# Constant rows written in 32-bit words on two engines, quotients of every head on ScalarE, and a newly searched order

## Chip, cores and metric

The kernel runs on one core of one Trainium2 chip. The metric is the device time of one execution in microseconds; of several runs the median counts. Engines are named TensorE (PE; PEld for its weight loads), VectorE (DVE), ScalarE (ACT), GpSimd (POOL) and SyncE (SP, which issues all the DMAs here). L448 means line 448 of the kernel before.

## What is computed

Eight batches of eight attention heads (1152 keys of 64 columns; queries averaged in pairs, so 576), followed by a channel mix with token shift on the 512 columns of each batch:

```python
q_pool = q.reshape(B, H, S // 2, 2, D).mean(axis=3)
scores = scale * np.matmul(q_pool, k.transpose(0, 1, 3, 2))
scores = scores - np.max(scores, axis=-1, keepdims=True)
attn = np.exp(scores); attn = attn / (np.sum(attn, axis=-1, keepdims=True) + 1e-09)
x = np.matmul(attn, v)                          # then heads side by side: (B, 576, 512)
...
xk = mu_k * x + (1.0 - mu_k) * x_prev
xr = mu_r * x + (1.0 - mu_r) * x_prev
k = np.maximum(xk @ w_k, 0.0)
v = k * k @ w_v
r = 1.0 / (1.0 + np.exp(-(xr @ w_r)))
return (r * v)
```

All is float32 outside; inside, each factor is a float16 value and a float16 remainder, so a product takes two or three matmuls.

## The kernel before

**Tiling.** The 64 heads (`n`) run one after the other, each in six blocks (`j`) of 96 queries against all 1152 keys (nine chunks of 128). A block computes scores into one of three PSUM banks `s` (L602), finds a maximum for each query on VectorE (for heads 0 to 13 in `row`, L612 to L622; from head 14 on in `top` and `join`, L627 to L648), adds the remainder products and the maximum (L653), takes exponentials on ScalarE into `pf` (L660) and has GpSimd make a scaled half-word copy `pl` (L663). `halves` (L712) and `window` (L741 to L748) multiply by the values into the one PSUM bank `a`. At the last window of a head the sums are divided: VectorE adds a guard and takes reciprocals (L764, L766), and the quotients `xb` are written by ScalarE for the first eight heads, one operation for each 128 queries (L769), and by one VectorE operation for the others (L773). After each second head the pair is turned: by a DMA transpose (`crossed`, L791 to L802) or on TensorE (`turns`, L818). When the eight heads of a batch are done, `mix` (L953 to L964) and `ff` (L985 to L1052) compute the channel mix in tiles of 256 tokens.

**Key buffers.** `ks1` holds, for each head, the keys and their remainders, turned; `ks2` (two buffers, used by even and odd heads) holds the keys once more in rows 64 to 127, copied there by a DMA (L551). Its rows 0 to 63 are written once, at the start: zeros, and two constants in rows 0 and 1, which multiply the maximum of a query.

**Order.** No engine works in program order of the source. Every operation is given to `op(engine, duration, function, reads, writes, key)`. A planner plays all of them with these durations and hand-over times, by key, refines the order in rounds, and then applies nudges (`MOVES`): each takes a centre in planned time, a width and a share of the operations there, and shifts their priorities. The result is one fixed order for each engine. The durations are used for the order alone. What stands outside `op` (identity, mask, gather, the fills of L442 to L456) is issued ahead of all that, in source order on its engine. SyncE's queue is in order, too: a DMA that waits holds those behind it.

The lines that the change and the steps below touch: the fills of `ks2` (L447 to L450), of `md` (L446), the casts into `gather` (L390), the subtraction for the key remainders (L540), the first query sums (L486), the quotients (L767 to L775), and the names `X_ACT`, `MOVES`, `SEED`, `GA`.

Of the kernel before, what the change touches and what calls it, by code (L numbers as in the profile page):

```python
# [4 lines left out]

# [6 lines left out]
F32 = mybir.dt.float32  # L12
# [27 lines left out]
CROSS = range(4, 31)  # L40
N_ROW = 14
PAIR = 99
GA = 0.045
XM = 3
SPLIT_ENG = 'ACT'
JOIN_ENG = 'ACT'
# [32 lines left out]
VB_DVE = 0  # L79
WHI_DVE = 0  # L80
VB_DUR = 0.25
X_ACT = 8
K_ONE = 2
Q_ONE = 2
N_QN = 2
# [2 lines left out]
WDEP = [("ks1", 1), ("ks2", 0), ("vr", 1)]  # L88
AHEAD2 = 0
MOVES, BASE, REACH = (  # L90
    34, 51, 119, 147, 174, 176, 191, 263, 328, 478, 600, 742, 785, 805, 941, 956, 1439, 1609, 3150, 4342,
    5377, 6334, 7410, 9224, 10224, 10571, 13731, 15873, 16751, 17268, 19136, 22188, 24107, 24376, 25583,
    25931, 31593,
), 2000000, 1150.0
SEED, SPREAD = 7, 1.0


class Issue:
# [224 lines left out]
def kernel(  # L323
# [63 lines left out]
    for a in range(P // U):  # L387
        part = slice(a * U, (a + 1) * U)
        nc.vector.memset(mask[part, a + 1:a + 2], 1.0 / SM)
        nc.gpsimd.tensor_copy(gather[part], ident[part, part].unsqueeze(1).broadcast_to([U, P // U, U]))  # L390
    nc.vector.memset(mask[0:U, 0:1], 1.0 / SM)

    kr, vr = bufs("kr", 2, [P, NC, D], F32), bufs("vr", 2, [P, NC, D], F32)
# [48 lines left out]
        nc.gpsimd.memset(t_[:, 1, :, 0:D], 0.0)  # L442
    for t_ in mx:
        nc.vector.memset(t_[:, 0:P - QN], 0.0)
    for t_ in md:
        nc.gpsimd.memset(t_, 0.0)  # L446
    for t_ in ks2:  # L447
        nc.vector.memset(t_[0:D], 0.0)  # L448
        nc.vector.memset(t_[0:2], -SM * 2.0 * EPS)
        nc.vector.memset(t_[0:1], -SM * (1.0 - EPS))  # L450
    for t_ in vt:
        nc.vector.memset(t_[:, :, 2 * D:2 * D + 2], 1.0)
    for t_ in vb:
# [128 lines left out]
    def block(n, j, i, t):  # L582

        hp, z = n % 2, i % 3
        qi = n // 2 % 2
        q0 = hp * TQ + j * QN
        qhi, qlo = (qT[qi][:, r].rearrange("p j x -> p (j x)")[:, q0:q0 + QN] for r in (0, 1))
        kh, kl = ([(t_, qi, c) for c in range(q0 // P, (q0 + QN - 1) // P + 1)] for t_ in ("qT", "qTl"))
        qm = [("qm", qi, q0)]
        s = s_b[z]  # L590
        p0 = (0 if hp else HW) + j * QN
        rows, us = slice(p0, p0 + QN), range(p0 // U, (p0 + QN) // U)

        def cols(c0, c1):
            return s[:, P + c0 * QN:P + c1 * QN]

        def grid(c0, c1):
            return cols(c0, c1).rearrange("p (c q) -> p c q", q=QN)

        def scores(c0, c1):  # L600
            for c in range(c0, c1):
                nc.tensor.matmul(cols(c, c + 1), ks1[hp][:, c, :], qhi,  # L602
                                 start=(c == c0), stop=False, skip_group_check=True)

        def first():
            for c0, c1 in BK:
                op("PE", (c1 - c0) * 0.0430, lambda c0=c0, c1=c1: scores(c0, c1),
                   r=[("ks1", hp), ("ks1", hp, 5)] + kh, w=[("s", z)], key=t)

        def row():  # L610
            mxz, mbz, y = mx[i % 2], mb[z], i % 2
            op("DVE", 0.975, lambda: nc.vector.tensor_reduce(mxz[:, P - QN:P], grid(0, NC).rearrange("p c q -> p q c"),  # L612
                                                             axis=AX.X, op=ALU.max),
               r=[("s", z)], w=[("mx", y)], key=t)
            op("PE", 0.059, lambda: nc.tensor.matmul(s[:, 0:P], mxz, identb, start=False, stop=False, skip_group_check=True),
               r=[("mx", y)], w=[("s", z)], key=t + O_MAX)
            op("DVE", 0.199, lambda: nc.vector.tensor_reduce(mbz, s[:, 0:P], axis=AX.X, op=ALU.max),
               r=[("s", z)], w=[("mb", z)], key=t + O_MAX)
            op("PE", 0.047, lambda: nc.tensor.matmul(s[:, 0:QN], mbz.broadcast_to([P, P]), negi[:, P - QN:P],
                                                     start=False, stop=False, skip_group_check=True),  # L620
               r=[("mb", z)], w=[("s", z)], key=t + O_MAX)
            op("ACT", 0.153, lambda: nc.scalar.activation(qlo[0:1], s[0:1, 0:QN], getattr(AF, ROW),  # L622
                                                          scale=(1.0 + EPS) / (1.0 - EPS), alpha=(1.0 - EPS) / (1.0 + EPS)),
               r=[("s", z)] + kl, w=qm, key=t + O_MAX)

        def top(y, a):
            op("DVE", 0.972, lambda: nc.vector.tensor_reduce(  # L627
                my[y][:, a], cols(0, NC).rearrange("p (x q) -> p x q", q=U), axis=AX.X, op=ALU.max, apply_transpose=True),
               r=[("s", z)], w=[("my", y)], key=t)

        def join(y, m):
            ql = qT[qi][0:U, 1].rearrange("p j x -> p (j x)")[:, q0 + QN - m * QN:q0 + QN]
            kls = kl if m == 1 else [("qTl", qi, c) for c in range((q0 - QN) // P, (q0 + QN - 1) // P + 1)]
            qms = [("qm", qi, q0 - x * QN) for x in range(m)]
            mr, got = s[:, 0:3 * m], s[0:U, U:U + 18 * m].rearrange("p (j k) -> p j k", k=6)
            mqz = mq[y][:, 0:3 * m]
            op("DVE", 0.062 + 0.028 * m, lambda: nc.vector.tensor_reduce(
                mr.rearrange("p (a j) -> p a j", j=3), my[y][:, 0:m].rearrange("p a (c j) -> p a j c", j=3), axis=AX.X, op=ALU.max),
               r=[("my", y)], w=[("s", z)], key=t + O_MAX)
            op("DVE", 0.061 + 0.019 * m, lambda: nc.vector.tensor_tensor(  # L640
                mqz, mr.unsqueeze(2).broadcast_to([P, 3 * m, 6]), mask.unsqueeze(1).broadcast_to([P, 3 * m, 6]), op=ALU.mult),
               r=[("s", z)], w=[("mq", y)], key=t + O_MAX)
            op("PE", GA, lambda: nc.tensor.matmul(s[:, U:U + 18 * m], gather.rearrange("p a x -> p (a x)"),
                                                  mqz.rearrange("p j k -> p (j k)"), start=False, stop=False, skip_group_check=True),
               r=[("mq", y)], w=[("s", z)], key=t + O_MAX)
            op("DVE", 0.055 + 0.031 * m, lambda: nc.vector.tensor_reduce(
                md[y][:, 0:3 * m, 0:2], windows(got, 5), axis=AX.X, op=ALU.max), r=[("s", z)], w=[("md", y)], key=t + O_MAX)
            op("DVE", 0.072 + 0.1 * m, lambda: nc.vector.transpose(ql, md[y][:, 0:3 * m].rearrange("p j x -> p (j x)")),  # L648
               r=[("md", y)] + kls, w=qms, key=t + O_MAX)

        def scores2(c0, c1):
            for c in range(c0, c1):
                nc.tensor.matmul(cols(c, c + 1), ks2[hp][:, c, :], qlo,  # L653
                                 start=False, stop=True, skip_group_check=True)

        def second():
            for c0, c1 in BK:
                op("PE", (c1 - c0) * 0.0430, lambda c0=c0, c1=c1: scores2(c0, c1),
                   r=[("ks2", hp)] + kl + qm, w=[("s", z)], key=t + O_EXP)
            op("ACT", NC * QN / 1200 + 0.06, lambda: nc.scalar.activation(  # L660
                pf[:, :, rows], grid(0, NC), AF.Exp, bias=SHIFT, scale=0.125 / (2.0 * SQ)),
               r=[("s", z)], w=[("pf", x) for x in us] + [("gate", i)], key=t + O_EXP)
            op("POOL", NC * QN / 1000 + 0.12, lambda: nc.gpsimd.tensor_scalar(  # L663
                pl[:, :, rows], half(pf, U16, 0)[:, :, rows], LO, 1.0, op0=ALU.mult, op1=ALU.mult),
               r=[("pf", x) for x in us], w=[("pl", x) for x in us], key=t + O_REST, port=True)

        return first, row, top, join, second

# [59 lines left out]
    def window(n, w, t):  # L728
# [37 lines left out]
        op("DVE", 0.08, lambda: nc.vector.reciprocal(dz, dz), r=[("den", z)], w=[("den", z)], key=t + O_EVAC)  # L766
        if n < X_ACT:  # L767
            for k_ in range(nk):
                op("ACT", 0.051 + D / 1200, lambda k_=k_: nc.scalar.activation(  # L769
                    xb[0][:, 2 * (k0 + k_) + hh], u[:, k_, 0:D], AF.Copy, scale=dz[:, k_:k_ + 1]),  # L770
                   r=[("den", z), ka], w=[("xb", 2 * (k0 + k_) + hh)], key=t + O_EVAC)
        else:
            op("DVE", 0.07 + nk * D / 960, lambda: nc.vector.tensor_tensor(  # L773
                xb[0][:, 2 * k0 + hh:2 * NW:2], u[:, :, 0:D], dz.unsqueeze(2).broadcast_to([P, nk, D]), op=ALU.mult),
               r=[("den", z), ka], w=[("xb", 2 * k_ + hh) for k_ in range(k0, NW)], key=t + O_EVAC)  # L775
# [2 lines left out]

    def copier(e, n):

        return {"POOL": (0.12 + n * 0.00113, nc.gpsimd.tensor_copy), "ACT": (0.093 + n / 1200, nc.scalar.copy),
                "DVE": (0.07 + n / 960, nc.vector.tensor_copy)}[e]

    def crossed(b, g, t):
# [268 lines left out]
        return key  # L1053


    queries(0, -20.0)
    prep(0, -20.0)
    prep(1, -10.0)
# [76 lines left out]
```

## Time and profile before

| | |
|---|---|
| median of 3 runs | 1095.19 us (1095.1 to 1096.24) |
| profiled execution | 1096.61 us, its span 1094.8 us |
| busy: TensorE, VectorE, ScalarE, GpSimd | 1052.2, 920.7, 878.2, 593.6 us |
| mean granted clock of TensorE | 0.995 |
| moved by DMA | 134.52 MB, mean 123 GB/s |

The span runs from the first to the last instruction of the profiled execution; the rest of its time lies around it. "Busy" of an engine is the time in which at least one of its instructions was under way. A row of a group gives busy time, mean duration, and after the second bar the idle time of the engine just before the group's instructions with what ended it ("<-").

### The profile page before, as it was taken

The numbers are of one execution on the slowest core, as the hardware profiler recorded it, in microseconds if no ns is written. First come the engines' busy times: TensorE is split into PE (matmuls) and PEld (weight loads), VectorE is DVE, ScalarE is ACT, GpSimd is POOL, SyncE is SP. The second block draws the span as 40 slices with busy tenths as digits, with TensorE's granted clock in tenths as the row PEclk, the third lists the DMA queues.
The fourth block names the chain that finished last, engine by engine and source line by source line (L and its number), as shares of the span: only waits on it lengthen the run. The fifth ranks groups of instructions, "written<-read, shape, count | busy, mean of one in ns | idle before, by whom it ended". The sixth has DMA issues, their size and how long they took to land.

```text
span 1094.8 us, 43933 instructions
## 1 busy us (share of the span) xinstructions
PE 1052.2 (96%) x18521; PEld 858.5 (78%) x18521; DVE 920.7 (84%) x2400; ACT 878.2 (80%) x1604; POOL 593.6 (54%) x641
## 2 busy tenths in 40 slices
PE   5888899999999999999999999999999999999998
PEld 4777887978688887888787888878787978787565
DVE  8889888989899989998998998998889899975321
ACT  6999998978778888888887788887788887865643
POOL 3556685645555464654565465656465645554431
PEclk9999999999999999999999999999999999999999
DMA  8998955666666538674675655565656654510000
GB/s 204 234 233 201 192 131 130 140 142 111 134 124 121 123 71 179 128 132 79 143 157 100 143 125 124 122 141 113 134 113 130 143 116 89 90 40 12 20 28 22
DMA packets 254166, 134.52 MB, mean 123 GB/s; under 512 B 189456, under 2 KB 226320, under 8 KB 253968
## 3 DMA queue, kind: packets, MB, share of 16 engines
q1 hardware_dynamic: 253968, 131.71, 57.6%
q8 instruction: 145, 2.38, 0.9%
q14 instruction: 53, 0.43, 0.1%
HBM read 67.11 MB, written 9.44 MB: 70 GB/s over the span
## 4 chain that ended last, share of the span: by engine, by line
PE 82%; ACT 5%; DVE 5%; DMA 2%; issue 2%; POOL 0%; ACTq 0%; DVEq 0%
PE f L985 34%; PE s L602 11%; PE s L653 11%; PE a L748 5%; PE a L743 5%; PE a L741 5%; PE s L985 5%; ACT pf L660 2%; PE a L712 2%; PE a L985 2%; DMA ks<-kn 2%; DVE my L627 1%; ACT xt L802 1%; DVE mx L612 1%; DVE xm L956 1%
## 5 line engine op out<-in xcount | busy, mean ns | idle before, releaser
L663 POOL TENSOR_SCALAR pl<-pf 128x864 f16<-128x864 uint16 x384 | 384.3, 1001 | 360.0 <-ACT pf L660 322.4
L660 ACT ACTIVATE pf<-s 128x864 int32<-128x864 f32 x384 | 335.1, 887 | 89.2 <-PE s L653 40.2
L627 DVE TRANSPOSE_TENSOR_REDUCE my<-s 128x27 f32<-128x864 f32 x300 | 319.9, 1072 | 48.7 <-PE s L602 35.9
L602 PE MATMUL s<-qT,ks 128*128 128x96 f16 x3456 | 216.7, 207 | 11.7 <-ACT pf L660 10.6
L653 PE MATMUL s<-qT,ks 128*128 128x96 f16 x3456 | 211.5, 207 | 3.8 <-ACT qT L622 2.9
L602 PEld LDWEIGHTS <-ks 128*128 128x128 f16 x3456 | 181.5, 98 | 41.4 <-issue 16.0
L653 PEld LDWEIGHTS <-ks 128*128 128x128 f16 x3456 | 177.6, 98 | 26.8 <-issue 5.1
L743 PE MATMUL a<-vt,pf 128*128 128x64 f16 x2304 | 192.0, 194 | 0.4 <-issue 0.4
L741 PE MATMUL a<-vt,pf 128*128 128x65 f16 x2304 | 191.5, 193 | 0.4 <-DVE xb L773 0.4
L741 PEld LDWEIGHTS <-pf 128*128 128x128 f16 x2304 | 160.1, 99 | 4.6 <-issue 0.7
L743 PEld LDWEIGHTS <-pf 128*128 128x128 f16 x2304 | 154.7, 98 | 6.4 <-issue 1.2
L985 PE MATMUL f<-xhk,wk_hi 128*128 128x256 f16 x496 | 135.0, 272 | 0.0
L985 PE MATMUL f<-xlk,wk_hi 128*128 128x256 f16 x496 | 135.0, 272 | 0.0
L985 PE MATMUL f<-xhk,wk_lo 128*128 128x256 f16 x496 | 135.0, 272 | 0.0
L748 PE MATMUL a<-vb,pl 128*128 128x65 f16 x2304 | 122.8, 193 | 0.1
L985 PEld LDWEIGHTS <-wk_hi 128*128 128x128 f16 x1152 | 105.0, 98 | 11.5 <-issue 0.5
L1016 POOL TENSOR_TENSOR gl<-g 128x512 f16<-128x512 f32 x72 | 78.9, 1097 | 55.5 <-ACT g L1014 53.6
L748 PEld LDWEIGHTS <-pl 128*128 128x128 f16 x2304 | 97.3, 98 | 6.0 <-POOL pl L663 0.3
L612 DVE TENSOR_REDUCE mx<-s 128x96 f16<-128x864 f32 x84 | 87.3, 1052 | 16.3 <-PE s L602 5.6
L985 PE MATMUL f<-wv_hi,g 128*128 128x512 f16 x240 | 90.8, 378 | 2.1 <-ACT ex L1033 2.0
L985 PE MATMUL f<-wv_lo,g 128*128 128x512 f16 x240 | 90.9, 379 | 0.0
L985 PE MATMUL f<-wv_hi,gl 128*128 128x512 f16 x240 | 90.9, 379 | 0.0
(130 smaller groups left out, 2095.1 us busy)
## 6 DMA issues: line engine op xcount, KB each, us to landing
kr<-in_k_dram SPq DMA_DIRECT2D x64, 288.0 KB
vr<-in_v_dram SPq DMA_DIRECT2D x64, 288.0 KB
qr<-in_q_dram SPq DMA_DIRECT2D x63, 256.0 KB
ks<-ks SPq DMA_DIRECT2D x64, 144.0 KB
out_dram<-em SPq DMA_DIRECT2D x36, 256.0 KB
xt<-in_moe_w_k_dram SPq DMA_DIRECT2D x8, 512.0 KB
xt<-in_moe_w_v_dram SPq DMA_DIRECT2D x8, 512.0 KB
qr<-in_q_dram SPq DMA_DIRECT2D x32, 64.0 KB
```

Source lines behind the costliest of these rows:

```text
L602: nc.tensor.matmul(cols(c, c + 1), ks1[hp][:, c, :], qhi, start=(c == c0), stop=False, skip_group_check=True)
L612: op("DVE", 0.975, lambda: nc.vector.tensor_reduce(mxz[:, P - QN:P], grid(0, NC).rearrange("p c q -> p q c"), axis=AX.X, op=ALU.max), r=[( ...
L627: op("DVE", 0.972, lambda: nc.vector.tensor_reduce(my[y][:, a], cols(0, NC).rearrange("p (x q) -> p x q", q=U), axis=AX.X, op=ALU.max, app ...
L653: nc.tensor.matmul(cols(c, c + 1), ks2[hp][:, c, :], qlo, start=False, stop=True, skip_group_check=True)
L660: op("ACT", NC * QN / 1200 + 0.06, lambda: nc.scalar.activation(pf[:, :, rows], grid(0, NC), AF.Exp, bias=SHIFT, scale=0.125 / (2.0 * SQ)) ...
L663: op("POOL", NC * QN / 1000 + 0.12, lambda: nc.gpsimd.tensor_scalar(pl[:, :, rows], half(pf, U16, 0)[:, :, rows], LO, 1.0, op0=ALU.mult, o ...
L712: nc.tensor.matmul(a_b[z * HW:(z + 1) * HW, x0:x1], tb[:, c, p0:p0 + HW], vs[(n - 1 + z) % NV][:, c, r0:r0 + x1 - x0], skip_group_check=Tr ...
L741: nc.tensor.matmul(bank[:, a0:a0 + VN], half(pf, F16, 1)[:, c, rows], vt[jv][:, c, D:D + VN], start=(w == 1 and c == 0 and hh == 0), stop= ...
L743: nc.tensor.matmul(bank[:, a0:a0 + D], half(pf, F16, 1)[:, c, rows], vt[jv][:, c, 0:D], start=False, stop=False, skip_group_check=True)
L748: nc.tensor.matmul(bank[:, a0:a0 + VN], pl[:, c, rows], vb[jv][:, c, 0:VN], start=False, stop=(c == NC - 1), skip_group_check=True)
L985: nc.tensor.matmul(ps, terms[i][0], terms[i][1], start=(first and i == 0), stop=(i == last), skip_group_check=True)
L1016: op("POOL", 2 * n * 0.00203 + 0.08, lambda f2=f2: nc.gpsimd.tensor_tensor(gl[:, f2, 0:n], g32[:, f2, 0:n], gh[:, f2, 0:n], op=ALU.subtrac ...
```

## The change

- The rows of zeros and constants of `ks2` are written through one function `rows`. A row's constant is packed twice into a 32-bit word, and the row is filled as 576 words and no longer as 1152 halves. VectorE fills buffer 0 in the same place as before; buffer 1 is filled by GpSimd, as an operation of the plan (key 10).
- The casts into `gather` and the fills of `md` on GpSimd become an operation of the plan too (key 60); the matmul that reads `gather` names it as read.
- `X_ACT` goes from 8 to 99: the quotients of every head are written by ScalarE, four or five operations of 64 columns each, and L773 is never used.
- `second` gets a branch that would make `pl` on ScalarE; `PL_J` is empty, so it is never taken.
- The planner's durations for the maxima, the join, the gather matmul (`GA`), ScalarE's quotients and one copy are changed, and so are the seed and the nudges, 60 in place of 37. These change the order of issue alone.

```diff
-GA = 0.045
+GA = 0.03
+PL_J = ()
-X_ACT = 8
+X_ACT = 99
 MOVES, BASE, REACH = (
-    34, 51, 119, 147, 174, 176, 191, 263, 328, 478, 600, 742, 785, 805, 941, 956, 1439, 1609, 3150, 4342,
...
+    1, 11, 127, 139, 152, 243, 284, 326, 402, 578, 644, 678, 752, 994, 1110, 1181, 1206, 1579, 1725, 2006,
...
 ), 2000000, 1150.0
-SEED, SPREAD = 7, 1.0
+SEED, SPREAD = 23, 1.0
...
     for a in range(P // U):
         part = slice(a * U, (a + 1) * U)
         nc.vector.memset(mask[part, a + 1:a + 2], 1.0 / SM)
-        nc.gpsimd.tensor_copy(gather[part], ident[part, part].unsqueeze(1).broadcast_to([U, P // U, U]))
...
-    for t_ in md:
-        nc.gpsimd.memset(t_, 0.0)
-    for t_ in ks2:
-        nc.vector.memset(t_[0:D], 0.0)
-        nc.vector.memset(t_[0:2], -SM * 2.0 * EPS)
-        nc.vector.memset(t_[0:1], -SM * (1.0 - EPS))
+    def rows(eng, t_):
+        eng.memset(t_[0:D], 0.0)
+        for r_, v_ in ((2, 2.0 * EPS), (1, 1.0 - EPS)):
+            two = struct.unpack("f", struct.pack("2e", -SM * v_, -SM * v_))[0]
+            eng.memset(t_[0:r_].rearrange("p c x -> p (c x)").bitcast(F32), two)
+
+    rows(nc.vector, ks2[0])
+
+    def later():
+        op("POOL", 2.2, lambda: rows(nc.gpsimd, ks2[1]), w=[("ks2", 1)], key=10.0)
+
+        def spread():
+            for a in range(P // U):
+                part = slice(a * U, (a + 1) * U)
+                nc.gpsimd.tensor_copy(gather[part], ident[part, part].unsqueeze(1).broadcast_to([U, P // U, U]))
+            for t_ in md:
+                nc.gpsimd.memset(t_, 0.0)
+
+        op("POOL", 1.7, spread, w=[("md", 0), ("md", 1), ("gather",)], key=60.0)
...
-               r=[("mq", y)], w=[("s", z)], key=t + O_MAX)
+               r=[("mq", y), ("gather",)], w=[("s", z)], key=t + O_MAX)
...
         if n < X_ACT:
             for k_ in range(nk):
-                op("ACT", 0.051 + D / 1200, lambda k_=k_: nc.scalar.activation(
+                op("ACT", 0.143 + D / 1200, lambda k_=k_: nc.scalar.activation(
                     xb[0][:, 2 * (k0 + k_) + hh], u[:, k_, 0:D], AF.Copy, scale=dz[:, k_:k_ + 1]),
...
-        return {"POOL": (0.12 + n * 0.00113, nc.gpsimd.tensor_copy), "ACT": (0.093 + n / 1200, nc.scalar.copy),
+        return {"POOL": (0.12 + n * 0.00113, nc.gpsimd.tensor_copy), "ACT": (0.093 + n / 1200 + (0.27 if n == 2 * (NW - 1) * P else 0.0), nc.scalar.copy),
...
+    later()
     queries(0, -20.0)
     prep(0, -20.0)
```

## Rows read from the trace of the kernel before

**Rows 1.** The page: busy us, share of the span, instructions by engine

```profile
PE 1052.2 (96%) x18521; PEld 858.5 (78%) x18521; DVE 920.7 (84%) x2400; ACT 878.2 (80%) x1604; POOL 593.6 (54%) x641
```

**Rows 2.** The page: the chain that ended last; the exponentials' group

```profile
PE 82%; ACT 5%; DVE 5%; DMA 2%; issue 2%; POOL 0%; ACTq 0%; DVEq 0%
...
L660 ACT ACTIVATE pf<-s 128x864 int32<-128x864 f32 x384 | 335.1, 887 | 89.2 <-PE s L653 40.2
```

**Rows 3.** Busy time by long stretches, its first line naming the columns

```profile
core 0: us, PE busy (x) PEld busy (x) DVE busy (x) ACT busy (x) POOL busy (x), PEclk, DMA share, GB/s
0.00:16.00 16.00, 5.66 (x74) 4.86 (x74) 12.84 (x39) 8.88 (x20) 3.91 (x16) 1.00 0.59 163
16.00:150.00 134.00, 114.93 (x2393) 102.33 (x2391) 118.26 (x207) 126.37 (x281) 84.47 (x87) 0.96 0.95 211
150.00:1000.00 850.00, 840.65 (x15477) 696.00 (x15475) 763.68 (x2113) 696.55 (x1208) 477.00 (x504) 1.00 0.59 119
```

**Rows 4.** The same table, columns as in rows 3, for short stretches early on

```profile
2.00:3.00 1.00, 0.00 (x0) 0.00 (x0) 0.70 (x2) 0.21 (x2) 0.85 (x4) 1.00 0.88 283
...
9.00:10.00 1.00, 1.00 (x11) 0.77 (x8) 0.60 (x2) 0.84 (x3) 0.00 (x0) 1.00 0.17 8
...
24.00:32.00 8.00, 6.53 (x146) 5.37 (x143) 7.60 (x14) 8.00 (x17) 2.79 (x3) 1.00 1.38 223
...
100.00:150.00 50.00, 44.95 (x888) 40.95 (x889) 43.61 (x75) 49.57 (x116) 35.66 (x37) 0.97 0.80 185
```

**Rows 5.** TensorE's waits (us, times, longest), 0 to 150; last row 150 to 1000

```profile
PE s L515 <- DVE kn L540: 8.5, 1, 8.5
...
PE s L602 <- ACT pf L660: 7.6, 19, 1.1
...
PE a L712 <- ACT xb L769: 0.5, 1, 0.5
...
PE s L602 <- ACT pf L660: 3.0, 6, 1.0
```

**Rows 6.** The start in order of time: start us, us, engine, line [idle before]

```profile
1.19 1.68 SPq L483 DMA_DIRECT2D qr<-in_q_dram  x3
...
1.48 0.54 DVE L448 MEMSET ks<- 64x576 uint32 x1
...
2.31 1.02 DVE L449 MEMSET ks<- 2x1152 f16 x1 [0.29 <-DVE ks L448]
...
3.58 0.77 ACT L537 CAST kn<-kr 128x320 f16<-128x320 f32 x2 [1.36 <-DMA kr<-in_k_dram]
...
6.85 1.02 DVE L450 MEMSET ks<- 1x1152 f16 x1 [0.29 <-DVE ks L449]
...
7.98 0.47 DVE L540 TENSOR_TENSOR kn<-kr,kn 128x320 f16<-128x320 f32 x1
...
16.93 2.16 POOL L663 TENSOR_SCALAR pl<-pf 128x864 f16<-128x864 uint16 x2 [12.02 <-ACT pf L660]
...
18.95 0.50 SPq L551 DMA_DIRECT2D ks<-ks  x1
```

**Rows 7.** Line 442's fills on GpSimd: ns min/median/max, first and last start

```profile
L442 POOL MEMSET qn<- x2: 577/577/577, 3.4 to 3.9; 128x576 f16 x2
```

**Rows 8.** Quotients: groups by form, five in time order, who waited for L773

```profile
L773 DVE TENSOR_TENSOR xb<-a,den 128x320 f32<-128x320 f32 x28 | 13.4, 478 | 0.3
...
L773 DVE TENSOR_TENSOR xb<-a,den 128x256 f32<-128x256 f32 x28 | 11.4, 407 | 0.3
...
L769 ACT ACTIVATE xb<-a,den 128x64 f32<-128x64 f32 x36 | 8.4, 291 | 0.0
...
71.91 1.08 ACT L769 ACTIVATE xb<-a,den 128x64 f32<-128x64 f32 x5
...
  ACT xp L791: 2.6, 4
...
  PE a L741: 0.4, 1
```

More of the change, by code (lines that the diff above doesn't have):

```diff
@@ L4 @@
 import random
+import struct
 import concourse.bass as bass
@@ L90 @@
 MOVES, BASE, REACH = (
-    34, 51, 119, 147, 174, 176, 191, 263, 328, 478, 600, 742, 785, 805, 941, 956, 1439, 1609, 3150, 4342,
-    5377, 6334, 7410, 9224, 10224, 10571, 13731, 15873, 16751, 17268, 19136, 22188, 24107, 24376, 25583,
-    25931, 31593,
[4 rows of a table added]
 ), 2000000, 1150.0
-SEED, SPREAD = 7, 1.0
+SEED, SPREAD = 23, 1.0
 class Issue:
@@ L626, in top @@
         def top(y, a):
-            op("DVE", 0.972, lambda: nc.vector.tensor_reduce(
+            op("DVE", 0.982, lambda: nc.vector.tensor_reduce(
                 my[y][:, a], cols(0, NC).rearrange("p (x q) -> p x q", q=U), axis=AX.X, op=ALU.max, apply_transpose=True),
@@ L636, in join @@
             mqz = mq[y][:, 0:3 * m]
-            op("DVE", 0.062 + 0.028 * m, lambda: nc.vector.tensor_reduce(
+            op("DVE", 0.07 + 0.028 * m, lambda: nc.vector.tensor_reduce(
                 mr.rearrange("p (a j) -> p a j", j=3), my[y][:, 0:m].rearrange("p a (c j) -> p a j c", j=3), axis=AX.X, op=ALU.max),
                r=[("my", y)], w=[("s", z)], key=t + O_MAX)
-            op("DVE", 0.061 + 0.019 * m, lambda: nc.vector.tensor_tensor(
+            op("DVE", 0.067 + 0.019 * m, lambda: nc.vector.tensor_tensor(
                 mqz, mr.unsqueeze(2).broadcast_to([P, 3 * m, 6]), mask.unsqueeze(1).broadcast_to([P, 3 * m, 6]), op=ALU.mult),
@@ L644, in join @@
                                                   mqz.rearrange("p j k -> p (j k)"), start=False, stop=False, skip_group_check=True),
-               r=[("mq", y)], w=[("s", z)], key=t + O_MAX)
-            op("DVE", 0.055 + 0.031 * m, lambda: nc.vector.tensor_reduce(
+               r=[("mq", y), ("gather",)], w=[("s", z)], key=t + O_MAX)
+            op("DVE", 0.063 + 0.031 * m, lambda: nc.vector.tensor_reduce(
                 md[y][:, 0:3 * m, 0:2], windows(got, 5), axis=AX.X, op=ALU.max), r=[("s", z)], w=[("md", y)], key=t + O_MAX)
-            op("DVE", 0.072 + 0.1 * m, lambda: nc.vector.transpose(ql, md[y][:, 0:3 * m].rearrange("p j x -> p (j x)")),
+            op("DVE", 0.08 + 0.1 * m, lambda: nc.vector.transpose(ql, md[y][:, 0:3 * m].rearrange("p j x -> p (j x)")),
                r=[("md", y)] + kls, w=qms, key=t + O_MAX)
@@ L662, in second @@
                r=[("s", z)], w=[("pf", x) for x in us] + [("gate", i)], key=t + O_EXP)
-            op("POOL", NC * QN / 1000 + 0.12, lambda: nc.gpsimd.tensor_scalar(
-                pl[:, :, rows], half(pf, U16, 0)[:, :, rows], LO, 1.0, op0=ALU.mult, op1=ALU.mult),
-               r=[("pf", x) for x in us], w=[("pl", x) for x in us], key=t + O_REST, port=True)
+            if n >= N_ROW and j in PL_J:
+                op("ACT", NC * QN / 1200 + 0.09, lambda: nc.scalar.activation(
+                    pl[:, :, rows], half(pf, U16, 0)[:, :, rows], AF.Copy, scale=LO),
+                   r=[("pf", x) for x in us], w=[("pl", x) for x in us], key=t + O_REST)
+            else:
+                op("POOL", NC * QN / 1000 + 0.127, lambda: nc.gpsimd.tensor_scalar(
+                    pl[:, :, rows], half(pf, U16, 0)[:, :, rows], LO, 1.0, op0=ALU.mult, op1=ALU.mult),
+                   r=[("pf", x) for x in us], w=[("pl", x) for x in us], key=t + O_REST, port=True)
         return first, row, top, join, second
```

3 rows, old and new, of the table AHEAD2 are left out of this document.

## Prediction

> **What bounds the kernel now.** I read the page first, then the table by stretches, then who waits for whom, and last the start in order of time. In the totals and slices [rows 1] the reader is to see that TensorE is the engine that is nearly always recorded busy, 1052.2 of 1094.8 us, so 42.6 us stand idle; VectorE (920.7) and ScalarE (878.2) are well filled, GpSimd (593.6) is half empty. The chain that ended last [rows 2] is 82% TensorE, so a gain has to remove TensorE's idle time. The table [rows 3] says where that lies: 10.3 us in the first 16 us (16.0 less 5.66), 19.1 in 16 to 150 (134.0 less 114.93), 9.4 in 150 to 1000 (850.0 less 840.65), and the rest, some 4, at the end. Matmuls are pipelined and recorded longer than the distance between them, so short gaps are hidden, and these sums are lower bounds of the losses.
>
> Two stages therefore have different limits. Up to 150 us the channel mix, which needs all eight heads of a batch, has little to give TensorE, and ScalarE sets the pace: busy 8.00 of 8 us in 24 to 32 and 49.57 of 50 in 100 to 150 [rows 4]. After 150 us TensorE is busy 840.65 of 850, ScalarE 696.55, VectorE 763.68 [rows 3]. There it waits little: the largest of its named waits in this stage is 3.0 us in 6 times, for the exponentials that free a score bank [rows 5].
>
> **The change part by part.**
>
> *Constant rows.* In the start in order of time [rows 6] VectorE writes the constants of both ks2 buffers from 1.48 to 7.87 us: per buffer one fill of 64 rows in 32-bit words (0.54), and two fills of 1152 halves (1.02 each), with 0.29 between dependent ones. The first subtraction for the keys (L540) stands behind them and starts at 7.98; its inputs were there much earlier, since the ScalarE cast of the same keys began at 3.58. TensorE stands idle 8.5 us for that L540 alone [rows 5]. After the change VectorE writes one buffer, and the two rows in 576 words each: 1.48 + 3 x 0.54 + 2 x 0.29 = 3.68, then the small fills that now lie between the last row's end at 7.87 and L540, so free at about 3.9. The cast of the first 320 columns ends at about 4.0 (3.58 + half of 0.77); with a hand-over of 0.2 (dependent fills on one engine show 0.29) the first L540 starts at 4.2: 3.8 us earlier. If a row filled in words still took 1.02, two would cost 0.96 more, and 2.9 were left. The first query sum (L486) needs its load of 128 KB, issued from 1.19 on, right behind the keys, which had landed by 3.58 [rows 6]; at 283 GB/s [rows 4] that is 0.5 us more, 4.1, so it does not hold. The loads pause at 9 to 10 us (8 GB/s [rows 4]) because SyncE's queue stands before a load into the key buffer that L540 frees, which moves forward too.
>
> *GpSimd's side.* It gains three fills of 576 words for the second buffer; the nearest row is its own fill of 576 halves at 0.577 us [rows 7]: 1.7 us, 2.3 with gaps of 0.29. Its casts for gather and its fills of md move behind them. It now stands idle 12.02 us before its first real work at 16.93 [rows 6], so all of that is covered: the new fills end before 7, while the transfer into that buffer is issued at 18.95 [rows 6]. gather and md serve heads from 14 on alone. Cost: nothing; without that cover, the 2.3 us.
>
> How much of the 3.8 us reaches the end? From 16 us on ScalarE is nearly full, and work that starts earlier ends earlier on a full engine; but the DMA engines show a share of 1.38 with 223 GB/s in 24 to 32 us [rows 4], and what waits for bytes does not move. Bounds 0 and 3.8; I take 3.5, near the upper one, since TensorE's 8.5 us wait is for VectorE and the loads pause right after it.
>
> *Quotients.* For heads 8 to 63, one multiplication on VectorE (28 of 320 columns at 478 ns, 28 of 256 at 407 [rows 8]) becomes five or four ScalarE operations of 64 columns, 252 in all. Five in a row take 1.08 us and one 0.291 [rows 8], so each next costs (1.08 - 0.29)/4 = 0.198. ScalarE gets 252 x 0.198 = 50 us, VectorE gives up 13.4 + 11.4 = 24.8 [rows 8]. They lie in 150 to 1000 us, where ScalarE has 153 us idle and VectorE 86 [rows 3]: ScalarE would go from 82% to 88%, VectorE from 90% to 87%. The bank of the attention sums is held longer: 1.08 against 0.48, and 0.88 against 0.41, mean 0.54 us, times 56 = 30 us if TensorE had nothing else ready. Now it waits for the quotient 0.4 us in one place [rows 8], because scores and channel mix stand ready behind. Queued behind the quotients on ScalarE are the exponentials (L660, 887 ns [rows 2]), which GpSimd and TensorE's score bank wait for. Against this, the copy xp no longer crosses engines (2.6 us of waits in 4 places [rows 8]), and VectorE, which is 5% of the chain [rows 2], is relieved. Bounds: a loss of 30, a gain of 9.4 (all idle time of that stage). I take a loss of 0.5, near the row that shows one wait of 0.4.
>
> The Trainium skill, "ScalarE: Activation LUTs", section "Rules for kernel authors", advises against this very move: multiplications belong on VectorE, not ScalarE. By operation the rows agree (0.48 against 1.08 us for 320 columns), and if engine time alone decided, the change would lose; the way it would is rival D.
>
> *Order.* Seed, 60 instead of 37 nudges and corrected durations give a new fixed order on every engine; PL_J is empty, so its branch never runs. The code draws three of four nudge centres from the first 170 us, where the idle time of 19.1 us lies [rows 3]. No row prices this. Bounds: a gain of those 19.1 us; a loss of the same size as the largest one-place waits, some six of 1.1 us [rows 5], 7 us. I take a gain of 2, a tenth of the idle time: the stage's limit, ScalarE's work, is not lessened by order, and its idle time in 16 to 150 us is only 7.6 us [rows 3].
>
> **Sum.** -3.5 + 0.5 - 2 = -5.0. The profiled execution took 1096.61 us with a span of 1094.8, so 1.8 lie around it; it stands 1.4 above the median of 1095.19. The span becomes 1089.8, the execution 1091.6, the median 1090.2.
>
> **The rivals.**
> B, order gives much: a third of the 19.1 us (6.4) and the whole 3.8 give -10.2, 1085. For it: most idle time is where the nudges are. Against: ScalarE's full slices there.
> C, the change doesn't bring its gain to the end: the early stage waits for bytes, not for VectorE, or the fills in words are no shorter, the quotients cost what they free, and order is worth nothing. Of the 3.8 us a fifth is left, -0.7, 1094.5. For it: the DMA share of 1.38; against: the pause at 9 to 10 us.
> D, slower, by one mechanism: ScalarE's five operations hold the attention bank and push the exponentials back while TensorE's next instruction needs one of them. Each exposed head costs 0.54 us; from 5.0/0.54, 9 of 56 heads, the gain is gone. With 17 exposed and no gain from order (-3.5 + 9.2 = +5.7 us) 1101. For it: ScalarE at 88%. Against: TensorE's order has channel mix between, and the eight first heads with this very form cost TensorE only one wait of 0.5 us (L712 for xb L769 [rows 5]). The skill's rule named above speaks for this rival.
>
> **How the numbers follow.** A 0.50, B 0.15, C 0.20, D 0.15. A and B are faster by over 0.2% (under 1093.0; 0.2% is about what a measurement of this kernel can tell from no change), C is within, D slower: 0.65, 0.20, 0.15. The range holds A and C, B to 1084 (a bit below its middle), and D's mild end: 1084 to 1098. A's own range is 1088 to 1092.5.
>
> **What would show it.** The first L540 near 4.2 us and the first matmul of L602 some 3.8 us earlier too; three ks fills of 0.54 us on VectorE; three on GpSimd before 7 us. No L773 at all, 288 of L769, ScalarE up by some 50 us. TensorE's idle time in 0 to 16 us down by 3 to 4, in 150 to 1000 us within 2 us of 9.4. B shows as idle time in 16 to 150 us below 14, C as TensorE reaching the stage of 150 us no earlier, D as waits of L741, L712 or L602 for L769 or L660 of 5 us and more. Wrong would be a lowered clock of TensorE in the late stage, where it is 1.00 now [rows 3], or a first query load that lands later than reckoned.

## The result, and the profile after

The changed kernel takes 1085.1 us (median of four runs, 1084.55 to 1086.6), against 1095.72 for the kernel before (four runs, 1095.1 to 1099.36). That is 10.6 us less where 5.0 were forecast; it lies inside the stated range (1084 to 1098), but the gain is more than twice the one reckoned. By the means of the runs the ratio is 0.9898, 95% interval 0.9874 to 0.9923, or 11.2 us less (8.4 to 13.8); the experiments below are given by such ratios. The profiled execution took 1084.55 us with a span of 1082.8, so the spans differ by 12.0. TensorE's mean granted clock was 0.995 in the profiled run before and 1.000 in this one. The clock does not make the gain, since the two other runs of the changed kernel at 0.995 took 1085.16 and 1086.6 us; it can be a part of the 12.0.

The first two groups of the page, busy time by engine and the chain that ended last (answering [rows 1] and [rows 2]):

```profile
PE 1048.3 (97%) x18521; PEld 856.0 (79%) x18521; DVE 899.8 (83%) x2341; ACT 926.4 (86%) x1856; POOL 598.4 (55%) x644
...
PE 87%; ACT 5%; DVE 4%; DMA 2%; issue 2%; SPq 0%; DVEq 0%; ACTq 0%
```

ScalarE is busy 48.2 us more (50 were reckoned), VectorE 20.9 less; TensorE's share of the chain has grown from 82% to 87%. The same stretches as in [rows 3] (columns named in the first line):

```profile
core 0: us, PE busy (x) PEld busy (x) DVE busy (x) ACT busy (x) POOL busy (x), PEclk, DMA share, GB/s
0.00:16.00 16.00, 8.63 (x88) 7.24 (x88) 11.12 (x39) 10.92 (x22) 6.64 (x20) 1.00 0.72 199
16.00:150.00 134.00, 114.20 (x2449) 101.03 (x2449) 122.25 (x208) 127.73 (x287) 89.08 (x90) 1.00 0.97 215
150.00:1000.00 850.00, 846.58 (x15493) 699.49 (x15491) 744.50 (x2065) 746.70 (x1466) 475.62 (x505) 1.00 0.57 118
```

TensorE's recorded idle time fell from 10.3 to 7.4 us in the first 16 us, rose from 19.1 to 19.8 in 16 to 150, and fell from 9.4 to 3.4 in 150 to 1000. The reader is to see that in the middle line, where the prediction placed the gain of the new order, TensorE stands idle as long as before, and in the late one, where it placed a small loss, 5.9 us less. The middle lines are not quite alike: their granted clock is 0.96 before and 1.00 after. Two stretches of the kernel before, each with its score matmuls, show what a lowered clock (0.50, which is 1.2 GHz and not 2.4) does to the records:

```profile
50.00:52.00 2.00, 2.00 (x28) 2.00 (x27) 2.00 (x3) 1.50 (x4) 0.81 (x1) 0.50 0.97 211
L602 PE MATMUL s<-qT,ks 128*128 128x96 f16 x9 | 0.9, 275 | 0.0
...
54.00:56.00 2.00, 2.00 (x66) 2.00 (x63) 1.92 (x3) 0.40 (x2) 1.60 (x2) 1.00 0.99 305
L602 PE MATMUL s<-qT,ks 128*128 128x96 f16 x9 | 0.5, 206 | 0.0
```

Neither stretch shows idle time, but nine matmuls of one shape take 0.9 us in one and 0.5 in the other. So idle time alone does not compare the two kernels before 150 us; the count of finished work further down does.

The start, in order of time (answering [rows 6]):

```profile
1.47 0.54 DVE L448 MEMSET ks<- 64x576 uint32 x1
...
2.19 0.54 DVE L451 MEMSET ks<- 2x576 f32 x1 [0.17 <-DVE ks L448]
...
2.90 0.54 DVE L451 MEMSET ks<- 1x576 f32 x1 [0.17 <-DVE ks L451]
3.11 1.05 POOL L448 MEMSET ks<- 64x1152 f16 x1
...
4.16 0.49 DVE L556 TENSOR_TENSOR kn<-kr,kn 128x320 f16<-128x320 f32 x1 [0.54 <-ACT kn L553]
4.22 1.19 POOL L451 MEMSET ks<- 2x576 f32 x2
...
6.42 0.46 ACT L553 CAST kn<-kr 128x320 f16<-128x320 f32 x1 [1.11 <-DMA kr<-in_k_dram]
6.78 0.69 ACT L536 COPY ks<-s 128x640 f16<-128x640 f16 x1
...
7.79 1.60 PE L618 MATMUL s<-qT,ks 128*128 128x96 f16 x18 [1.51 <-ACT qT L536]
...
15.54 1.91 POOL L684 TENSOR_SCALAR pl<-pf 128x864 f16<-128x864 uint16 x2 [8.27 <-ACT pf L676]
```

The first subtraction (L540 before, L556 now) starts at 4.16, as reckoned (4.2). The first score matmul (L602 before, L618 now) comes at 7.79, 2.8 us earlier than the 10.63 of before, and not at some 6.8: ScalarE has the cast of head 1's keys ahead of the copies that release it, and that cast stands 1.11 us for its load. GpSimd's fills are covered, with 8.27 us of idle time left.

Now the quotients, one group by form and all of TensorE's named waits from 150 to 1000 us (us in total, times, longest; answering [rows 5] and [rows 8]):

```profile
L790 ACT ACTIVATE xb<-a,den 128x64 f32<-128x64 f32 x288 | 69.6, 320 | 6.3 <-DVE den L787 4.4 <-DVE md L662 1.2 <-DVE mq L656 0.7
```

```profile
PE s L659 <- DVE mq L656: 1.2, 3, 0.5
PE f L1006 <- DVE em L1070: 0.9, 2, 0.6
PE f L1006 <- ACT r L1033: 0.5, 1, 0.5
PE s L618 <- ACT pf L676: 0.5, 2, 0.3
```

No wait for the 252 new operations is among them, and the wait for the exponentials has gone from 3.0 to 0.5 us.

**Where the lead is won.** Recorded waits hide gaps shorter than a matmul's recorded length (0.206 us for 96 columns). So the table counts TensorE's finished work: every matmul that has started by a given time, at the distance to the next that the traces show for its size at the full clock (0.042 us for 96 columns, 0.109 for 256, 0.216 for 512; columns/2400 + 0.0027 us fits these). The difference of the sums at one time is the lead of one kernel over another, in us:

| lead over the kernel before, at | 16 | 150 | 300 | 600 | 900 | 1000 us |
|---|---|---|---|---|---|---|
| changed kernel | 0.7 | 4.2 | 5.7 | 9.7 | 9.6 | 11.7 |
| only the fills (e1) | 1.4 | 4.1 | 4.5 | 4.9 | 4.5 | 4.5 |
| order and quotients, old fills (e5) | -0.2 | 0.7 | 2.2 | 5.9 | 6.1 | 8.2 |
| only the quotients (e2) | -0.4 | 0.2 | -2.1 | -10.5 | -21.8 | -23.8 |

The lead of e1 is that of one of its four fastest runs (1091.6 to 1092.2 us; the other eight took 1093.8 to 1095.7). A third of the gain is there at 150 us and belongs to the fills: e1 has it too. It is not the clock's: from 16 to 150 us e1 had a granted clock of 0.97, hardly more than the 0.96 of the kernel before. The rest comes between 150 and 600 and between 900 and 1000 us, where the granted clock is 1.00 in all of them.

### The profile page after: what moved, and what is told of

The parts are those of the page before. It is cut to its first block, busy times and chain, and to the rows that moved or that the text cites. A ratio compares the mean times of both kernels' runs of the same rounds, so it can differ in the third digit from the quotient of the medians.

```text
span 1082.8 us, 44147 instructions
## 1 busy us (share of the span) xinstructions
PE 1048.3 (97%) x18521; PEld 856.0 (79%) x18521; DVE 899.8 (83%) x2341; ACT 926.4 (86%) x1856; POOL 598.4 (55%) x644
## 4 chain that ended last, share of the span: by engine, by line
PE 87%; ACT 5%; DVE 4%; DMA 2%; issue 2%; SPq 0%; DVEq 0%; ACTq 0%
PE f L1006 36%; PE s L618 12%; PE s L669 12%; PE a L769 6%; PE a L764 6%; PE a L762 6%; PE s L1006 5%; PE a L733 2%; ACT pf L676 2%; PE a L1006 2%; DVE mx L628 1%; DVE my L643 1%; DMA qT<-qn 1%; ACT xb L790 1%; DMA vr<-in_v_dram 0%
## 5 line engine op out<-in xcount | busy, mean ns | idle before, releaser
L618 PE MATMUL s<-qT,ks 128*128 128x96 f16 x3456 | 214.6, 206 | 10.0 <-ACT pf L676 7.4
L618 PEld LDWEIGHTS <-ks 128*128 128x128 f16 x3456 | 179.8, 98 | 35.0 <-issue 12.2
L764 PE MATMUL a<-vt,pf 128*128 128x64 f16 x2304 | 190.4, 194 | 0.0
L764 PEld LDWEIGHTS <-pf 128*128 128x128 f16 x2304 | 154.1, 97 | 6.0 <-issue 0.2
L769 PE MATMUL a<-vb,pl 128*128 128x65 f16 x2304 | 120.1, 193 | 0.2 <-POOL pl L684 0.2
L769 PEld LDWEIGHTS <-pl 128*128 128x128 f16 x2304 | 94.9, 97 | 5.0 <-POOL pl L684 0.3
```

Of the source, the lines that this page charges most:

```text
L618: nc.tensor.matmul(cols(c, c + 1), ks1[hp][:, c, :], qhi, start=(c == c0), stop=False, skip_group_check=True)
L764: nc.tensor.matmul(bank[:, a0:a0 + D], half(pf, F16, 1)[:, c, rows], vt[jv][:, c, 0:D], start=False, stop=False, skip_group_check=True)
L769: nc.tensor.matmul(bank[:, a0:a0 + VN], pl[:, c, rows], vb[jv][:, c, 0:VN], start=False, stop=(c == NC - 1), skip_group_check=True)
```

## The experiments

Each ratio is to the kernel before on the same chip, with its 95% interval; us are the ratio's difference from 1 times 1096. By the intervals such a figure is good to some 1.5 us, for e2 and e3 to 2.4, for the changed kernel to 2.7. The theories: **O**, the new order brings most, and the parts add up; **Q**, the quotients on ScalarE bring most; **J**, the parts pay only together with an order made for them.

**One part at a time, in a fixed order (e1 to e6).** In these the issue order of every engine is that of the kernel before or of the changed kernel, instruction by instruction, and only the part named differs. A quotient that changes its engine stands where its counterpart stood.

Fills of the change in the kernel before:

```diff
-    for t_ in ks2:
-        nc.vector.memset(t_[0:D], 0.0)
...
+    rows(nc.vector, ks2[0])
+    rows(nc.gpsimd, ks2[1])
```

> The kernel before, with its fixed order kept on every engine; only the constant rows are filled as in the change (VectorE fills buffer 0 in words, GpSimd buffer 1, gather and md behind them). Theory O (the new order brings most of the gain, the parts add up): 1092.5, that is -3 for the fills. Theory Q (the quotients on ScalarE bring most): -3 too, 1092.5. Theory J (the parts pay only together with an order made for them): within 1 us of before, 1095, because the order's next bottleneck in the early stage takes the 3.8 us back.

Measured: 0.9976 (0.9963 to 0.9989), -2.6 us. The fills are worth about what they were taken for, without any new order; J falls for them.

Quotients of the change in the kernel before:

```diff
-            op("DVE", 0.07 + nk * D / 960, lambda: nc.vector.tensor_tensor(
...
+            op("DVE", 0.07 + nk * D / 960, lambda: [nc.scalar.activation(
+                xb[0][:, 2 * (k0 + k_) + hh], u[:, k_, 0:D], AF.Copy, scale=dz[:, k_:k_ + 1]) for k_ in range(nk)],
```

> The kernel before, order kept; the quotients of heads 8 to 63 are written by ScalarE at the place where the VectorE operation stood. Theory O: within 1.5 us of before (1094 to 1097). Theory Q: 4 to 6 us less, about 1090. Theory J: slower by 2 us and more, since ScalarE's queue was not laid out for it.

Measured: 1.0239 (1.0217 to 1.0261), +26 us. TensorE's waits from 150 to 1000 us in this kernel (us in total, times, longest), and its line of the same stretch:

```profile
PE s L602 <- ACT pf L660: 8.8, 20, 0.8
PE a L712 <- ACT xb L773: 5.6, 10, 1.3
PE a L741 <- ACT xb L773: 4.7, 9, 1.0
```

```profile
150.00:1000.00 850.00, 823.18 (x15024) 678.06 (x15023) 732.92 (x2015) 723.76 (x1413) 456.04 (x490) 1.00 0.57 119
```

TensorE stands idle 26.8 us in this stretch (850.0 less 823.18), against 9.4 in [rows 3]. The attention bank is waited for in 19 places where [rows 8] had one, and the exponentials in 20 where [rows 5] had six. Each head's guard addition (L764) can be paired with its quotients and with the next matmul into the bank: in 26 of the 53 heads of this stretch TensorE's next use of the bank starts within 0.15 us of the last quotient; in the kernel before in 3 of 54, in the changed one in 4 of 55. Both halves of rival D are there, the bank that is held and the exponentials that are pushed back. Its price of 0.54 us for each exposed head accounts for 14 of the 26 us; the waits for the exponentials grew by 5.8 (3.0 to 8.8), and the rest no named wait shows. That the loss comes near D's upper bound of 30 us is thus in part chance.

Both of these edits in the kernel before:

> The kernel before, order kept, both parts. Theory O: 1092.5, the rest of the 10.6 us (some 7.5) being the order's. Theory Q: 1087 to 1088. Theory J: 1095 to 1098.

Measured: 1.0227 (1.0205 to 1.025), +24.9 us: the quotients' loss, with a gain of the fills (1.3) too small to be told from noise here. O and Q fall; J has the sign, but its 1095 to 1098 falls too.

The changed kernel's order with both parts undone:

```diff
-                    xb[0][:, 2 * (k0 + k_) + hh], u[:, k_, 0:D], AF.Copy, scale=dz[:, k_:k_ + 1]),
+                    ...) if n < 8 else nc.vector.tensor_tensor(...) if k_ == 0 else None,
...
-        op("POOL", 2.2, lambda: rows(nc.gpsimd, ks2[1]), w=[("ks2", 1)], key=10.0)
+        op("POOL", 2.2, lambda: None, w=[("ks2", 1)], key=10.0)
```

> The changed kernel's order kept on every engine, with both parts undone: fills as before on VectorE in halves, quotients of heads 8 to 63 by one VectorE operation at the place of the first ScalarE one. Theory O: 1088, that is -7.5 by the order alone. Theory Q: 1093 to 1094. Theory J: 1093 to 1096, the order without its parts is no better than the old one.

Measured: 1.0007 (0.9992 to 1.0021): nothing. O and Q fall, J holds: with the old parts put back, the new order is no better than the old one. But VectorE's quotients then stand in queues that were laid out without them, so this is not what an order planned for the old parts would give.

The changed kernel with the old fills, and with the old quotients (one each of these two edits):

> The changed kernel, order kept, with the fills of the kernel before (VectorE, halves, both buffers). Theory O and theory Q: the fills are worth 3 us, so 1088. Theory J: more is lost than the 3.8 us of the delay itself, 1089 and up.

Measured: 0.9929 (0.9913 to 0.9945), -7.8 us, so the fills bring 3.4 of the 11.2 (good to some 3 us). The 1088 of O and Q holds; J falls for the fills again (1088.6, not 1089 and up, and no more lost than the 3.8).

> The changed kernel, order kept, with the quotients of heads 8 to 63 back on VectorE at the place of the first ScalarE one. Theory O: within 1.5 us of the changed kernel, 1084 to 1086.5. Theory Q: 4 to 6 us more, 1089 to 1091. Theory J: 2 us and more above the changed kernel.

Measured: 0.9994 (0.9983 to 1.0005), -0.7 us: put back on VectorE in this order, the quotients cost 10.5 us. J holds; Q has the sign and half the size. Its waits from 150 to 1000 us, on TensorE and on ScalarE, and its line of that stretch:

```profile
PE a L733 <- DVE xb L791: 1.8, 4, 0.5
...
PE a L762 <- DVE xb L791: 1.1, 4, 0.4
```

```profile
ACT pf L676 <- PE s L669: 39.6, 46, 3.4
...
ACT xp L814 <- DVE xb L791: 12.5, 13, 1.7
```

```profile
150.00:1000.00 850.00, 840.60 (x15433) 694.55 (x15430) 760.86 (x2110) 698.42 (x1201) 474.85 (x501) 1.00 0.57 118
```

TensorE waits for the quotients here 2.9 us in eight places, yet it stands idle 9.4 us in all, 6.0 more than in the changed kernel. ScalarE's queue stands 12.5 us in 13 places before the copy xp, for a product that VectorE, in its own fixed queue, delivers late (2.6 us in 4 places in [rows 8]). Its exponentials wait 39.6 us for TensorE's scores, against 27.7 in the changed kernel and 37.8 in the kernel before. These waits fit a delay that passes from VectorE to ScalarE and on to TensorE, but no row shows the whole chain.

The six together, in us against the kernel before:

| | old quotients | new quotients |
|---|---|---|
| old order, old / new fills | 0 / -2.6 | +26.2 / +24.9 |
| new order, old / new fills | +0.8 / -0.7 | -7.8 / -11.2 |

The fills bring 1.3 to 3.4 us in all four pairs, though only 2.6 and 3.4 are clear of noise. Order and quotients do not add up: the quotients alone cost 26 us, the order alone gives nothing, and together they give 7.8. That is what J says, for these two.

**Planned anew, without nudges (e7 to e12, e15, e16).** A fixed order punishes whatever is swapped under it. So the next kernels let the planner make the whole order for the part, with an empty list of nudges.

```diff
 MOVES, BASE, REACH = (
-    1, 11, 127, 139, 152, 243, 284, 326, 402, 578, 644, 678, 752, 994, 1110, 1181, 1206, 1579, 1725, 2006,
...
 ), 2000000, 1150.0
```

> The kernel before with an empty list of nudges: the planner's order after its rounds alone. If the nudges bring real time, this is some 5 us slower than before (1100 and more); if they only fit the plan's own numbers, within 2 us of it.

Measured: 0.9999 (0.9987 to 1.0012). The 37 nudges of the kernel before bring nothing that a measurement shows.

> The changed kernel with an empty list of nudges (its seed, its durations, both parts). If the search is what brings the gain, this is near the kernel before without nudges less the parts' 3 us, 1097 or so, some 10 us above the changed kernel; if seed and corrected durations bring it, within 3 us of the changed kernel, 1085 to 1088.

Measured: 0.9949 (0.9935 to 0.9963), -5.6 us. This lies between the two forecasts: half of the changed kernel's gain is there without nudges, the other half (5.6 us, good to some 3) is theirs. Of the first half the fills can be some 3 us; no run takes them out of this order.

The place of the quotients then, for three seeds with the change's fills and durations (`X_ACT` 8 or 99), and for the plan of the kernel before (there with the change's duration for ScalarE's quotient, old fills). The theories: **P**, ScalarE is the better place once the order is planned for it; **S**, it is the draw of the order. The edits, beside the empty list, one or both:

```diff
-X_ACT = 99
+X_ACT = 8
...
-SEED, SPREAD = 23, 1.0
+SEED, SPREAD = 7, 1.0
```

> The changed kernel without nudges and with the quotients of heads 8 to 63 planned and written on VectorE (X_ACT 8), so that the whole order is planned for that; to be compared with the changed kernel without nudges (0.9949 of before, 1089.7). Theory P (ScalarE is the better place once the order is planned for it, since VectorE is the fuller engine after 150 us): 3 to 5 us slower than that, 1093 to 1095. Theory S (seed and luck of the order make the difference, the place does not matter): within 1.5 us of it, 1088 to 1091.

> The kernel before without nudges (0.9999 of before, 1095.5), with the quotients of all heads planned and written on ScalarE at the duration of the change; old fills, other durations and seed as before. Theory P: 3 to 5 us faster than without, 1091 to 1093. Theory S: within 1.5 us of 1095.5. In neither the 26 us that the same move cost in the old fixed order.

> The changed kernel without nudges and with the seed of the kernel before (7 in place of 23). Theory P: within 2 us of the same with seed 23 (1088 to 1092). Theory S: several us away from it, up to 1095.

> The same with seed 7 and the quotients of heads 8 to 63 planned on VectorE. Theory P: 3 to 5 us slower than the one with seed 7 and ScalarE. Theory S: no fixed sign, within 1.5 us or faster.

> The changed kernel without nudges and with a third seed, 5. Theory S (an unsearched order scatters by some 5 us either way): anywhere from 1089 to 1102, and 23 was a good draw. Theory P (the plan with ScalarE's quotients is better as such): below 1092, and the 1101.6 of seed 7 was a bad draw.

> The same with the quotients of heads 8 to 63 planned on VectorE, seed 5. Theory P: 3 to 8 us slower than its partner. Theory S: sign open; with the pairs of seeds 23 (+8.7), 7 (-5.8) and the old plan (-3.7) the mean of the place is then near zero.

| measured, no nudges | VectorE | ScalarE | ScalarE less VectorE |
|---|---|---|---|
| seed 23 (e9, e8) | 1.0024 (1.0012 to 1.0036) | 0.9949 (0.9935 to 0.9963) | -8.2 us |
| seed 7 (e12, e11) | 0.9999 (0.9984 to 1.0014) | 1.0045 (1.0023 to 1.0067) | +5.0 us |
| seed 5 (e16, e15) | 0.9959 (0.9944 to 0.9974) | 1.0045 (1.0028 to 1.0062) | +9.4 us |
| plan of before (e7, e10) | 0.9999 (0.9987 to 1.0012) | 1.0030 (1.0014 to 1.0047) | +3.4 us |

Each difference is good to 2 or 3 us (e16's expectation has three of them by medians, and as VectorE less ScalarE). P falls: in three of four pairs ScalarE is the worse place. S holds in that the sign is not fixed, but its "within 1.5 us" fell in e9 and e10, and e11 came out slower than either theory had it. The 26 us of e2 are gone in all pairs. With the order planned for it, the place of the quotients makes -8 to +9 us, and kernels with the quotients in the same place scatter as widely (0.9949 to 1.0045 on ScalarE, 0.9959 to 1.0024 on VectorE). The change has the one seed of three in which ScalarE came out ahead.

**The nudges (e13, e14, e17, e18).** The 27 nudges with their centre in the first 170 us, and the 33 others:

```diff
 MOVES, BASE, REACH = (
+    243, 284, 402, 752, 1110, 1181, 1725, 2006, 2055, 2638, 2742, 2881, 3381, 4637, 7647, 9754, 11021, 11047,
+    11323, 11758, 12027, 13307, 14244, 14354, 35663, 45917, 48084,
```

> The changed kernel with the 27 of its 60 nudges whose centre lies in the first 170 us of the plan. Without nudges it took 1089.7, with all 1085.1. Theory E (the nudges repair the early stage, as the prediction took it): this one keeps nearly all of the 5 us, 1085 to 1086.5. Theory L (the gain comes from the late stage, where the late nudges act, or from any reordering): half of it or less, 1088 and more, and the lead over the kernel without nudges grows after 150 us, not before.

> The changed kernel with the other 33 nudges alone, centres from 200 to 970 us of the plan. Theory E: as without nudges, 1089 to 1091. Theory L: 1086 to 1088.

Measured: 0.9933 (0.9916 to 0.995) and 0.9929 (0.9914 to 0.9944), 1.8 and 2.2 us less than without nudges (each good to some 2.4, so neither is clear of noise), and 5.6 with all. Theory E falls: the early half does not keep nearly all of the gain, and its lead over the kernel without nudges is -0.2 us at 150 us and +1.6 at 1000. L's "half or less" fits, though the late half, at 1089.0, came out a little above its 1086 to 1088. A nudge in the first 170 us of the plan can shift every choice after it, and what little it brings here comes later.

Then two orders with the quotients on VectorE and nudges of their own, 45 for seed 5 and 54 for seed 23, each kept because it shortened the plan:

```diff
-X_ACT = 99
+X_ACT = 8
 MOVES, BASE, REACH = (
-    1, 11, 127, 139, 152, 243, 284, 326, 402, 578, 644, 678, 752, 994, 1110, 1181, 1206, 1579, 1725, 2006,
...
-SEED, SPREAD = 23, 1.0
+SEED, SPREAD = 5, 1.0
```

> The changed kernel with the quotients of heads 8 to 63 planned on VectorE, seed 5, and 45 nudges of its own, searched in the same way as the change's (each kept because it shortens the plan). Without nudges it was 0.9959 of before, 1092.2. Theory R (nudges found with the corrected durations bring real time, wherever the quotients are): 3 to 6 us less, 1086 to 1089, close to the changed kernel without ScalarE's quotients. Theory F (nudges mostly fit the plan, and the 5.6 us of the changed kernel's were a lucky draw): 1091 to 1093.

> The same with seed 23 and 54 nudges of its own; without nudges 1.0024 of before, 1098.4. Theory R: 3 to 6 us less, 1092 to 1095. Theory F: within 2 us of 1098.

Measured: 0.9959 (0.9942 to 0.9977), no change against e16; and 0.9968 (0.9955 to 0.9981), 6.1 us less than e9. So of four lists of nudges two bring about 6 us (the change's, and that of e18) and two nothing (those of the kernel before and of e17). F holds for e17 and R for e18, so neither holds as a rule. No kernel of this study is faster than the changed one.

## Why the prediction was wrong, point by point

- **Fills: right.** L540 at 4.16 us (4.2 reckoned). Worth 2.6 us in the old order and 3.4 in the new one (3.5 reckoned), 4.1 to 4.9 in the lead of e1 from 150 us on. The first score matmul came 2.8 us earlier and not 3.8. GpSimd's side costs nothing, and its three fills took 2.3 us in all (3.11 to 5.41), as reckoned, but by other parts: the fill of the 64 rows took 1.05 us and not 0.577; its row has 1152 elements where VectorE's has 576.
- **ScalarE's load: right.** 48.2 us for 50.
- **Quotients: the term "a loss of 0.5" failed, because it was priced alone.** The step took the one wait of 0.4 us in [rows 8] for the size of the loss. That wait belongs to VectorE's operations of 0.41 to 0.48 us, in an order made for them: with ScalarE's operations in the same place half of the heads had no cover left, and the kernel lost 26 us (e2), near the upper bound and by rival D's mechanism. A wait that a fixed order leaves over says nothing of the slack that it has hidden. In the changed kernel no wait for a quotient is left, so there the term cannot be told apart from the order's.
- **Order: the term "a gain of 2" failed, in size and in place, and this is the step that made the forecast too small.** It was put into 16 to 150 us, since TensorE's idle time lies there and the code draws three of four nudge centres there; of the 60 nudges kept, only 27 have theirs there. Idle time in that stretch went from 19.1 to 19.8 us, and without the fills the new order with its quotients had a lead of 0.7 us at 150 us and 8.2 at 1000 (e5). In 150 to 1000 us, where idle time was to stay within 2 us of 9.4, it fell to 3.4. Order and quotients together give 7.8 us where the sum had 1.5 (2 less 0.5). As two terms they cannot be added: measured apart, the quotients cost 26 us and the order gives 0.
- **What was luck.** The measured time lies in the range because the range was drawn down to 1084 for rival B, not because the sum or its mechanism came near.
- **The rivals.** B has the measured time (1085) by the wrong way: its sign was to be idle time below 14 us in 16 to 150. C's lead that never arrives was not seen: the lead of 4.2 us at 150 us stays. D happened in e2 and e3, and in the changed kernel none of its waits is left.
- **The rule of the Trainium skill** ("ScalarE: Activation LUTs", section "Rules for kernel authors"): multiplications go to VectorE and not to ScalarE. With the order planned for either place, the kernel was faster that way in three of four pairs (by 3.4 to 9.4 us), and slower by 8.2 us with the change's seed.
- **What stays open.** Why seed 23 with its 60 nudges keeps TensorE so well fed, and whether a search as long as the change's would bring VectorE's quotients to the same time. The runs show a scatter of about 5 us either way between the eight orders without nudges, of which the change's (e8) is the best; they don't show a reason that could have been read from the trace of before.

## What to carry to other kernels

Where every engine's order is fixed ahead, an operation that is moved has no price of its own, since what hides it belongs to one order. Here the same move cost 26 us in the old order, saved 10.5 in the new one, and made -8 to +9 us when the order was planned for it. So keep its full exposed length as the upper end for the old order, and ask whether the order is made anew. Test parts in a frozen order and in one planned for them: the first shows which terms are tied to the order (here the quotients, not the fills), the second whether the part or the draw of the order wins. A new search of an order is a term of its own, with a scatter that only runs of several draws show, and it need not pay in the stretch where its nudges lie.

## What the runs showed of the hardware beyond that

VectorE filled 1152 halves of zeros as 576 words even before the change (0.54 us), but constants as 1152 halves (1.02 us), and constants packed into words in 0.54; GpSimd took 1.05 us for the 1152 halves of zeros and 1.19 for two fills of 576 words. On ScalarE the 64-column quotient was recorded with 291 ns on average, yet five in a row took 1.08 us [rows 8] and not 1.46, so its recorded length overstates what it takes from the engine.
